# TensorE's last part of the usual path: beside the branch, or behind the general path

## Chip, cores, metric

One core of one Trainium2 chip. The metric is the device time of one execution in microseconds (us); lower is better. Eight executions took 561.7 to 562.5 us at a mean granted clock of 0.997; where a text below says "full clock", these are left out and runs at 0.999 or 1.000 are kept.

## The reference, cut

An adaLN-conditioned block over 2,048 rows of width 512, in bf16: attention (32 query heads of 128, grouped over 8 cached heads, the last 512 keys) and then an MLP. Only the second matters here.

```python
def _B_ref(x, w1, w2):                       # D = 512, Dff = 1792
    h = jnp.einsum('bsd,df->bsf', x, w1)
    h = jnp.maximum(h, zero)
    return jnp.einsum('bsf,fd->bsd', h, w2)
...
h = _layernorm(x, axis=-1) * (1 + cb) + sb
x = x + gb * _B_ref(h, B_w1, B_w2)
```

## The kernel before

The kernel has a fast path, which skips the softmax's maximum, and a general path. During the fast path it works out whether the values were in range: a count of 128 good partitions, written to `flag`. Each engine has a cut in its list of operations; there it waits for the flag, loads it into a register and tests it. With 128 it runs its last part, otherwise the last part and then the general path. TensorE's cut lies in the MLP, ahead of the last two of the four `y_group`s (14 matmuls each) of the second of four blocks of rows.

```python
def emit(self, stream, eng, lo=0, hi=None):
    for fn, waits, incs in stream.ops[lo:hi]:
        for k, c in waits:
            eng.wait_ge(self.sems[k], c)
        ins = fn(eng)
        for k, n in incs:
            ins.then_inc(self.sems[k], n)
...
mlp.extend(lambda b=b, tl=tl: y_group(b - 1, tl) for tl in range(TPB))
if b == NB - 2:
    mlp.insert(len(mlp) - 2, lambda: cut_here("pe"))
    mlp.extend(lambda n=n: cut_here(n) for n in ("dve", "sp", "pool"))
...
# the last y group goes out in three pieces
mlp.extend(lambda a=a: y_group(NB - 1, TPB - 1, *a) for a in
           ((0, D // 2, ACT), (D // 2, 3 * D // 4, SP), (3 * D // 4, D, ACT)))
...
def engine(name, e):
    stream, n_ops = fast[name], cut[name]
    kb.emit(stream, e, 0, n_ops)
    e.wait_ge(sems[flag_ev[0]], flag_ev[1])
    v = e.value_load(flag[0:1, 0:1])
    ...                                # last_part() and rerun(), see the diff
    if name == "pe":
        with e.If(v == 128):
            last_part()                # next to the branch
        with e.Else():
            rerun()                    # the general path
    else:
        with e.If(v != 128):
            rerun()
        with e.Else():
            last_part()                # behind the general path
```

The order of the source is the order of the instructions. So TensorE falls through at the test and has a far jump, over the general path, behind its last matmul; the other four engines jump far at the test (their records of it last 50 to 72 ns) and have the end of the block next to their last part.

Of the kernel before, what the change touches and what calls it, by code (L numbers as in the profile page):

```python
# [1811 lines left out]
def bass_adaLN_cond__sliding_block_cached__dense_activation_relu__prompt_kernel(  # L1812
    nc: bass.Bass,
    A_x: bass.AP,
    A_k_cache: bass.AP,
    A_v_cache: bass.AP,
    A_wq: bass.AP,
    A_wo: bass.AP,
    B_x: bass.AP,
    B_w1: bass.AP,  # L1820
    B_w2: bass.AP,
    c: bass.AP,
    w_mod: bass.AP,
    out: bass.AP,
):
    args = (A_x, A_k_cache, A_v_cache, A_wq, A_wo, B_x, B_w1, B_w2, c, w_mod, out)
    with ExitStack() as top:
        flag = top.enter_context(nc.sbuf_tensor("flag", [1, 8], mybir.dt.int32))
        with ExitStack() as es:
            kb, fast, cut, dma_cnt, flag_ev = build_fast(nc, es, top, *args, flag)  # L1830
            sems = dict(kb.sems)
            meet = top.enter_context(nc.semaphore("s_meet"))
        with ExitStack() as es:
            gkb, general = build_general(nc, es, *args)

            def engine(name, e):
                stream, n_ops = fast[name], cut[name]
                kb.emit(stream, e, 0, n_ops)
                e.wait_ge(sems[flag_ev[0]], flag_ev[1])
                v = e.value_load(flag[0:1, 0:1])  # L1840

                def last_part():
                    kb.emit(stream, e, n_ops)

                def rerun():
                    kb.emit(stream, e, n_ops)
                    if stream.cnt:
                        e.wait_ge(sems[name], stream.cnt)
                    if name == "sp":
                        for k, n in dma_cnt.items():  # L1850
                            e.wait_ge(sems[k], n)
                    e.sem_inc(meet, 1)
                    e.wait_ge(meet, len(fast))
                    gkb.emit(general[name], e)

                if name == "pe":
                    with e.If(v == 128):
                        last_part()
                    with e.Else():
                        rerun()  # L1860
                else:
                    with e.If(v != 128):
                        rerun()
                    with e.Else():
                        last_part()

            with nc.allow_non_contiguous_dma(reason="tiny c vector load in column layout, value rows of 256 bytes"):
                with nc.Block() as block:
                    @block.sync
                    def _(e):  # L1870
                        engine("sp", e)

                    @block.tensor
                    def _(e):
                        engine("pe", e)

                    @block.scalar
                    def _(e):
                        engine("act", e)

                    @block.vector
                    def _(e):
                        engine("dve", e)

                    @block.gpsimd
                    def _(e):
                        engine("pool", e)
    return nc
# [28 lines left out]
```

## Time and profile before

| | kernel before |
|---|---|
| median of 3 runs (range) | 560.84 us (560.29 to 560.89) |
| span of the profiled execution | 558.9 us |
| TensorE busy, granted clock | 98%, 1.0 |
| TensorE's branches | 509.9 us: 90 ns; 554.6 us: 3610 ns |

The time is the device's; the span runs from the first to the last instruction of the profiled execution and is about 2 us shorter.

### The profile page before, as it was taken

Reading aid. Unit: us, or ns where it says so; the run is one execution under the profiler, and the core shown is the slowest. Engines: PE = TensorE matmul, PEld = TensorE weight load, DVE = VectorE, ACT = ScalarE, POOL = GpSimd, SP = SyncE. Lnnn points to the kernel's source line nnn. Section 1 sums busy time; section 2 is a strip of 40 time slices with the busy share of each in tenths; the row PEclk is TensorE's granted clock in tenths of the full one; section 3 lists DMA queues with packets and bytes.
Section 4 is the critical chain, followed back from the end, with each engine's and each line's share of the span. In section 5 each row is a group of like instructions: output and inputs, shape, how many; then the busy total and the mean of one; then the engine's idle time right before and its main releaser. Section 6 shows DMA issues by size and latency. Waiting matters only on the chain.

```text
span 558.9 us, 9675 instructions
## 1 busy us (share of the span) xinstructions
PE 549.5 (98%) x4061; PEld 315.5 (56%) x4135; DVE 254.7 (46%) x555; ACT 349.3 (63%) x453; POOL 53.3 (10%) x50
## 2 busy tenths in 40 slices
PE   8999999999999999999999999999999999999997
PEld 4665555555555555555555555555555554444444
DVE  4455555553546544335445443333354438322134
ACT  5986666666666666666666666666666644432500
POOL 2000022004410000033000000332000000000000
PEclk9999999999999999999999999999999999999999
DMA  9999662522225144353352412121214110200001
GB/s 258 257 203 192 137 162 47 114 43 73 39 41 74 39 84 106 62 129 58 95 95 56 76 40 39 39 38 38 39 39 76 39 29 0 49 28 22 21 29 48
DMA packets 113357, 42.66 MB, mean 76 GB/s; under 512 B 93977, under 2 KB 112153, under 8 KB 113305
## 3 DMA queue, kind: packets, MB, share of 16 engines
q1 hardware_dynamic: 112584, 41.08, 35.5%
q10 hardware_dynamic: 720, 0.89, 0.5%
q8 instruction: 33, 0.54, 0.4%
q14 instruction: 20, 0.16, 0.1%
HBM read 18.35 MB, written 2.10 MB: 37 GB/s over the span
## 4 chain that ended last, share of the span: by engine, by line
PE 97%; issue 1%; DVE 1%; DMA 1%; POOL 0%
PE psS L1374 28%; PE psO L1374 27%; PE psQ L1374 23%; PE psW L1374 19%; DMA x<-in_A_x_dram 1%; DVE st L1384 0%; POOL xn L1613 0%; POOL rstd L1596 0%; DVE mv L1385 0%; DVE qT L1620 0%; PE psS L1377 0%; DVE rstd L1593 0%; DVE PT L1734 0%; DVE PT L1736 0%; DVE tmp L1424 0%
## 5 line engine op out<-in xcount | busy, mean ns | idle before, releaser
L1498 ACT ACTIVATE PT<-psS 128x1024 bf16<-128x1024 f32 x256 | 262.7, 1028 | 128.7 <-PE psS L1374 128.5
L1374 PE MATMUL psS<-qT,kT 128*128 128x512 bf16 x510 | 151.4, 379 | 0.3 <-DVE qT L1620 0.2
L1374 PEld LDWEIGHTS psO<-v,PT 128*128 128x128 bf16 x2048 | 126.6, 98 | 30.2
L1374 PE MATMUL psO<-v,PT 128*128 128x129 bf16 x2048 | 137.0, 220 | 0.0
L1374 PE MATMUL psQ<-hT,wq 128*128 128x512 bf16 (+1 forms) x509 | 130.2, 377 | 0.2
L1508 DVE RECIPROCAL rinv<-psO 128x4 f32<-128x4 f32 x128 | 23.3, 182 | 225.6 <-PE psO L1374 225.6
L1374 PE MATMUL psW<-wo,oT 128*128 128x512 bf16 x452 | 118.1, 379 | 3.1
L1509 DVE TENSOR_TENSOR o<-psO,rinv 128x512 bf16<-128x512 f32 x128 | 88.5, 691 | 4.5
L1374 PEld LDWEIGHTS psQ<-hT,wq 128*128 128x128 bf16 x512 | 49.9, 98 | 59.8 <-DVE qT L1488 0.4
L1374 PEld LDWEIGHTS psS<-qT,kT 128*128 128x128 bf16 x512 | 49.6, 98 | 58.8 <-ACT PT L1498 0.5
L1490 ACT ACTIVATE qT<-psQ 128x512 bf16<-128x512 f32 x125 | 74.1, 593 | 0.0
L1723 ACT ACTIVATE wq<-psS 128x512 bf16<-128x512 f32 x56 | 33.4, 597 | 49.1 <-PE psS L1374 49.1
L1374 PEld LDWEIGHTS psW<-wo,oT 128*128 128x128 bf16 x512 | 44.9, 98 | 32.9 <-DVE acc L1531 1.2
L1531 DVE TENSOR_TENSOR acc<-psW,acc 128x512 f32<-128x512 f32 x48 | 33.2, 691 | 6.7 <-PE psW L1374 6.7
L1374 PE MATMUL psO<-wmw,wq 128*128 128x512 bf16 (+1 forms) x165 | 32.8, 352 | 0.2
L1534 POOL TENSOR_TENSOR acc<-acc,gaf 128x512 f32<-128x512 f32 x12 | 15.6, 1301 | 146.8 <-DVE acc L1531 139.8
L1390 POOL TENSOR_TENSOR rstd<-rstd,cst 128x4 f32<-128x4 f32 x7 | 7.2, 1025 | 215.7 <-DVE rstd L1389 215.7
L1734 DVE TENSOR_TENSOR PT<-psO,gbf 128x512 f32<-128x512 f32 (+1 forms) x12 | 7.5, 624 | 40.4 <-PE psO L1374 40.4
L1374 PE MATMUL psS<-h2T,wmw 128*128 128x512 bf16 x110 | 25.2, 379 | 0.1
L1374 PEld LDWEIGHTS psO<-wmw,wq 128*128 128x128 bf16 x168 | 15.3, 98 | 16.6
L1374 PE MATMUL psS<-hT,wmw 128*128 128x512 bf16 x110 | 24.4, 379 | 0.1
L1384 DVE BATCH_NORM_STATS2 st<-x 128x6 f32<-128x512 bf16 x31 | 21.1, 680 | 3.6 <-DMA x<-in_A_x_dram 3.6
(90 smaller groups left out, 192.0 us busy)
## 6 DMA issues: line engine op xcount, KB each, us to landing
wo<-in_A_wo_dram SPq DMA_DIRECT2D x4, 1024.0 KB, 6.5
wq<-in_A_wq_dram SPq DMA_DIRECT2D x7, 512.0 KB, 4.6
wmw<-in_B_w_dram SPq DMA_DIRECT2D x14, 256.0 KB, 3.1
wmw<-in_w_mod_dram SPq DMA_DIRECT2D x4, 512.0 KB, 5.1
oT<-o SPq DMA_TRANSPOSE x128, 2.4
out_dram<-PT SPq DMA_DIRECT2D x15, 128.0 KB, 1.7
x<-in_A_x_dram SPq DMA_DIRECT2D x3, 512.0 KB, 4.4
v<-in_A_v_cache_dram SPq DMA_DIRECT2D x8, 128.0 KB, 4.1
```

The lines of the kernel that those rows point to most:

```text
L1374: kb.op(PE, lambda e: e.matmul(out_ap, lhsT, rhs, start=start, stop=stop), reads=reads, group_writes=[R_b[k] for k in bk], signal=signal)
L1384: kb.op(DVE, lambda e: e.bn_stats(st[:, t, :], x_sb[:, t, :]), reads=[R_x[t]], writes=[R_st[t]])
L1390: kb.op(POOL, lambda e: e.tensor_tensor(rstd[:, sl], rstd[:, sl], cst[:, 0:1].to_broadcast([P, hi - lo]), op=ALU.pow), reads=R_rstd[sl] + ...
L1490: kb.op(ACT, lambda e: e.activation(qT[u % NQT][:, :], bank[bk], ACTF.Copy), reads=[R_b[bk]], writes=[R_qT[u % NQT]])
L1498: kb.op(ACT, lambda e: e.activation(PT[u % NPT][:, pr * 2:pr * 2 + 2, :], s_ps[pr][:, :, :], ACTF.Exp, scale=scale), reads=[R_b[pr * 2], R ...
L1508: kb.op(DVE, lambda e: e.reciprocal(rinv[:, u, :], o_ps[:, :, P]), reads=[R_b[5], R_b[6]], writes=[R_rinv])
L1509: kb.op(DVE, lambda e: e.tensor_tensor(o_sb[u % NOS][:, :, :], o_ps[:, :, 0:P], rinv[:, u, :].unsqueeze(2).to_broadcast([P, TPB, P]), op=A ...
L1531: kb.op(DVE, lambda e: e.tensor_tensor(acc[:, tl, :], bank[WBK], acc[:, tl, :], op=ALU.add), reads=[R_b[WBK], R_acc[tl]], writes=[R_acc[tl]])
L1534: kb.op(eng, lambda e: e.tensor_tensor(acc[:, tl, :], acc[:, tl, :], gaf[:, :], op=ALU.mult), reads=[R_acc[tl], R_ga], writes=[R_acc[tl]])
L1723: kb.op(ACT, lambda e: e.activation(h1T[b % 2][:, fc, :], bank[bk], ACTF.Relu), reads=[R_b[bk]], writes=[R_h1[b % 2][fc]], pre=all_events( ...
L1734: kb.op(DVE, lambda e: e.tensor_tensor(yt[i][:, c0:c1], bank[bk][:, c0:c1], gbf[:, c0:c1], op=ALU.mult), reads=[R_b[bk], R_gb], writes=[R_ ...
```

## The change

Its intent is a simpler program: TensorE gets the same layout as the others. The usual path then pays for one far jump of TensorE in the MLP, and for none at the end.

```diff
--- before.py
+++ after.py
@@ -1838,11 +1838,7 @@
                 kb.emit(stream, e, 0, n_ops)
                 e.wait_ge(sems[flag_ev[0]], flag_ev[1])
                 v = e.value_load(flag[0:1, 0:1])
-
-                def last_part():
-                    kb.emit(stream, e, n_ops)
-
-                def rerun():
+                with e.If(v != 128):
                     kb.emit(stream, e, n_ops)
                     if stream.cnt:
                         e.wait_ge(sems[name], stream.cnt)
@@ -1852,17 +1848,8 @@
                     e.sem_inc(meet, 1)
                     e.wait_ge(meet, len(fast))
                     gkb.emit(general[name], e)
-
-                if name == "pe":
-                    with e.If(v == 128):
-                        last_part()
-                    with e.Else():
-                        rerun()
-                else:
-                    with e.If(v != 128):
-                        rerun()
-                    with e.Else():
-                        last_part()
+                with e.Else():
+                    kb.emit(stream, e, n_ops)
 
             with nc.allow_non_contiguous_dma(reason="tiny c vector load in column layout, value rows of 256 bytes"):
                 with nc.Block() as block:
```

No arithmetic, wait or transfer of data changes; the list of TensorE's instructions before and behind the branch is the same in both kernels.

## The prediction

Where a cut is marked, a passage is gone: on how instructions are stored and fetched, on the depth of a queue, and on the clock. The forecast's sum: 0.99 + 1.0 + 1.37 = 3.36 us of jump, or 3.61 as measured, gives a gap of 0.21 or 0.46 us, 0.35 is chosen, and 560.84 + 0.35 = 561.2 us. Part (a), why the target must be fetched: for that stand only the packets that the trace has behind the far branches (the one inside the jump at the end: 16 KB, 1.25 us).

> **What bounds the kernel now.** I read the page first: engine totals, then the chain that ended last.
>
> ```profile
> PE 549.5 (98%) x4061; PEld 315.5 (56%) x4135; DVE 254.7 (46%) x555; ACT 349.3 (63%) x453; POOL 53.3 (10%) x50
> PEclk9999999999999999999999999999999999999999
> PE 97%; issue 1%; DVE 1%; DMA 1%; POOL 0%
> ```
>
> TensorE is busy 98% of 558.9 us at an undiminished clock, and 97% of the chain of waits is its own matmuls. So any time in which its array really runs dry goes straight into the end, and nothing that only delays another engine by a microsecond matters. The change touches one place on TensorE: the test of the flag inside the MLP. So I next read the instructions of the flag, of the lines of the two branches, and of the block's end (columns: line, engine queue, operation, count, durations in ns as min/median/max, first and last start in us).
>
> ```profile
> L1840 PEldq TENSOR_LOAD <-flag x1: 488/488/488, 509.4 to 509.4; - x1
> L1857 PEldq COMPARE_BRANCH  x2: 90/1850/3610, 509.9 to 554.6; - x2
> L1862 ACTq COMPARE_BRANCH  x1: 50/50/50, 508.2 to 508.2; - x1
> L1862 DVEq COMPARE_BRANCH  x1: 72/72/72, 520.8 to 520.8; - x1
> L1862 SPq COMPARE_BRANCH  x1: 53/53/53, 521.9 to 521.9; - x1
> L1868 PEldq DRAIN  x1: 68/68/68, 558.3 to 558.3; - x1
> L1868 SPq DRAIN  x1: 13/13/13, 558.6 to 558.6; - x1
> ```
>
> TensorE has two branches now. The first, at 509.9 us, is not taken: it falls through into the last part and takes 90 ns. The second, at 554.6 us, is the jump over the general path to the end of the block, and its record lasts 3610 ns. That is a far jump of this very engine, measured in this very kernel, only at a place where it stands beside the drain of the last results. The last row but one and the last show that TensorE arrives at the end at 558.3 us and SyncE, which waits for the last output, at 558.6 us: the far jump of today costs nothing, by 0.3 us.
>
> Third, the timeline of TensorE around the test (start, length, engine, instructions).
>
> ```profile
> 506.97 5.93 PEld L1374 LDWEIGHTS psO<-wmw,wq 128*128 128x128 bf16 x28
> 507.18 6.21 PE L1374 MATMUL psO<-wmw,wq 128*128 128x512 bf16 x27
> 513.01 2.04 PEld L1374 LDWEIGHTS psQ<-wmw,wq 128*128 128x128 bf16 x10
> 513.23 2.10 PE L1374 MATMUL psQ<-wmw,wq 128*128 128x512 bf16 x9
> ```
>
> The load and the branch at 509.4 to 510.0 us leave no trace on the array. It works through 28 matmuls of psO without a gap until 513.23 us, and only then comes psQ, the first matmul behind the branch. So the sequencer is ahead of the array: when it reads the flag (509.363 us in the trace), the array has (513.228 - 509.363) / 0.216 = 18 matmuls to go, 3.87 us. The same lead of some 18 matmuls is there at the end of the kernel, where a matmul of 128 columns starts every 56 ns: (555.75 - 554.62) / 0.056 = 20. So the lead is a queue that is full, and the sequencer can fill it at 28 ns an instruction or faster.
>
> [...]each far branch is followed by a packet of the instruction queues, and TensorE's record of 3610 ns contains one.[...]the trace shows a lead of 18 pairs of weight load and matmul, 36 instructions, and I use the 36.[...]
>
> **The change, part by part.** No arithmetic, wait, load of the flag or transfer of data changes. Three things do.
>
> (a) The branch at 509.9 us is now taken, and its target lies behind the general path. Counted in the compiled program of the kernel before, TensorE's general path has 5,942 instructions and its last part 448[...].
>
> (b) The jump at the end goes: the last part now lies next to the end of the block. 3.61 us of sequencer time disappear, but from a place with 0.3 us less than SyncE's arrival. Gain: 0.
>
> (c) The other four engines already have this layout, and stay.
>
> The cost of (a) is the far jump less the lead. The jump I take apart with the instruction packets, by windows of the DMA view (queue, packets, MB, share of 16 engines' time in the window): the first line is the window 555.6 to 557, the second 510.97 to 511.9, an ordinary fetch in sequence with little traffic beside it.
>
> ```profile
> q8 instruction: 1, 0.02, 5.6%
> q8 instruction: 1, 0.02, 6.2%
> ```
>
> A share times 16 times the window is the packet's time: 0.056 x 16 x 1.4 = 1.25 us, and 0.062 x 16 x 0.93 = 0.92 us. The packet of the far jump started at 555.61 us, 0.99 us after the branch did (554.62), landed at 556.86, and the record ended at 558.23, 1.37 us later. The other engines have the same first step (from their branch to a packet on their instruction queue: DVE 1.02 us, SyncE 0.96 us, ACT 0.99, POOL 1.37), so it is the jump and not the drain of TensorE's queue that sets it. In the middle of the MLP the packet should be like the ordinary ones, most of which take 0.92 to 1.15 us. Sum: 0.99 + 1.0 + 1.37 = 3.36 us; or, as measured once, 3.61.
>
> The branch starts at 509.915. The sequencer goes on at 509.915 + 3.36 = 513.28 (513.53 with the other figure). Between the end of the jump at the kernel's end and the next instruction 0.06 us pass, and a weight load takes 98 ns, so psQ's first matmul can start at 513.28 + 0.06 + 0.10 = 513.44 (513.69). It started at 513.228. **The array runs dry for 0.21 us (0.46 us)**; everything else of the 3.4 us lies under the 15 matmuls in the queue. I choose 0.35, between the two.
>
> Behind it nothing is regained: the last part is one chain of matmuls at 216 ns, and the tail (last eviction, last output, SyncE's waits) shifts with it. The queue refills, since 28 ns an instruction is well below the 108 ns at which the array takes one. The prediction is 560.84 + 0.35 = 561.2 us.
>
> **The rivals.**
>
> First: the lead hides it wholly. If the fetch comes back faster (a packet of 0.9 us, or a resume in less than 1.37 us because that step held something of the kernel's end), the jump takes under 3.2 us and the change costs nothing: 560.8 us. For it: the margin is only 0.2 us. Against: the only jump of this engine that was measured took 3.61 us.
>
> Second: a second fetch on top. [...]in the kernel before, the fetch in sequence began at 510.98, just 1 us behind the branch. If the sequencer has that block already under way when it jumps, the wanted packet stands behind a useless one of about 1 us, and the loss is 0.35 + 1.0: 562.2 us. ACT's jump shows two packets in a row (508.83 and 509.17), which may be just this.[...]
>
> Third: no lead, the whole jump exposed, since the sequencer must drain before it branches: 560.84 + 3.6 = 564.4 us[...]. Against it: in the kernel before, the load and branch ran 3.2 us ahead of the array, and the packet at the end began at its usual 1.0 us.
>
> Fourth: a gain from the end, if TensorE's arrival there were what the others wait for. Against it: SyncE arrives 0.3 us later, and it waits for the last output, which ACT issued at 556.45 us, after VectorE; 560.84 or better is not expected from this.
>
> **Range and chances.** The runs of the kernel before spread from 560.29 to 560.89, so half a microsecond is noise. The first rival gives 560.5 to 560.9, the main line 561.0 to 561.4, the second up to 562.2. I weigh them 0.25, 0.5 and 0.15, with a rest of 0.1 for the third and the unknown. A range of 560.5 to 562.2 holds the most of it. Two per cent are 11.2 us, three times a whole far jump: same is almost certain.
>
> **What would show it.** Right: TensorE has one far branch, at 509.9 us, of 3.3 to 3.6 us, with one instruction packet of 16 KB starting about 510.9; psQ's first matmul starts 0.2 to 0.5 us after the psO group has ended, where there was no gap; TensorE reaches the drain of the end near 556 us instead of 558.3; SyncE still ends last. Wrong: no gap at all (first rival); two packets of the instruction queue before psQ (second); a gap of over 3 us[...] (third); or an end that comes earlier relative to the last matmul (fourth).

## More of the kernel before

A change of the time by tenths of a microsecond is to be read from two stretches of the span: the MLP around 510 us, and the tail, from VectorE's last write (556.42 us) to the last instruction. The prediction shows the lines of the first. In the second, the outputs leave in pieces; the following lines are the last pieces in the DMA view of the kernel before (output, queue of the issuing engine, operation, count, KB, us from issue to landing).

```profile
out_dram<-PT SPq DMA_DIRECT2D x15, 128.0 KB, 1.7
out_dram<-PT ACTq DMA_DIRECT2D x1, 64.0 KB, 2.7
out_dram<-PT SPq DMA_DIRECT2D x1, 32.0 KB, 2.4
out_dram<-PT ACTq DMA_DIRECT2D x1, 32.0 KB, 1.9
```

A piece of 128 KB lands in 1.7 us (a median of 15), and the later piece of half the size takes 2.7.

## The result

| | before | changed |
|---|---|---|
| median of 6 runs (range) | 560.75 us (560.29 to 560.90) | 560.69 us (560.46 to 560.85) |
| span of the profiled execution | 558.855 us | 558.965 us |

The ratio is 1.0, with a 95% interval of 0.9987 to 1.0012: the same. (A ratio is the mean time of one kernel's fast runs over that of the other's of the same rounds, so not quite the ratio of the medians quoted.) The time is inside the predicted range, 0.5 us under the predicted value. The profile says that this equality has two parts that were not both foreseen.

The lines of the branches and the block's end, changed kernel:

```profile
L1841 PEldq COMPARE_BRANCH  x1: 3860/3860/3860, 509.8 to 509.8; - x1
L1841 ACTq COMPARE_BRANCH  x1: 50/50/50, 508.1 to 508.1; - x1
L1855 PEldq DRAIN  x1: 1195/1195/1195, 555.2 to 555.2; - x1
L1855 SPq DRAIN  x1: 13/13/13, 558.7 to 558.7; - x1
```

The far jump has moved to 509.8 us and takes 3.86 us. TensorE now reaches the end at 555.2 us (its drain lasts until 556.4), SyncE as before last, at 558.7. The timeline of TensorE around the branch, changed kernel (in brackets the idle time of the row's first instruction):

```profile
506.90 5.92 PEld L1374 LDWEIGHTS psO<-wmw,wq 128*128 128x128 bf16 x28
513.75 1.19 PEld L1374 LDWEIGHTS psQ<-wmw,wq 128*128 128x128 bf16 x7 [0.93 <-issue]
507.11 6.21 PE L1374 MATMUL psO<-wmw,wq 128*128 128x512 bf16 x27
513.76 1.47 PE L1374 MATMUL psQ<-wmw,wq 128*128 128x512 bf16 x6 [0.44 <-issue]
```

There is a hole where the kernel before had none. The row's 0.44 us is counted from the modelled end of a matmul (379 ns); in a stream a matmul starts every 216 ns, so by starts the hole is 513.758 - (512.938 + 0.216) = 0.604 us. I use this measure below and call it the gap. Everything behind it comes 0.54 us later than before (VectorE's last write ends at 556.96 instead of 556.42 us; the stretch ahead of the branch had come 0.07 us earlier). But the span grew by only 0.11 us. The rest is given back in the tail, which took 2.438 us before and takes 2.005 us now. The last pieces of the output, changed kernel:

```profile
out_dram<-PT SPq DMA_DIRECT2D x15, 128.0 KB, 1.7
out_dram<-PT ACTq DMA_DIRECT2D x1, 64.0 KB, 1.6
out_dram<-PT SPq DMA_DIRECT2D x1, 32.0 KB, 1.5
out_dram<-PT ACTq DMA_DIRECT2D x1, 32.0 KB, 1.5
```

All three land sooner, the 64 KB by 1.1 us. The DMA view of the kernel before for the window 554.5 to 558.8 us has one line that the changed kernel's tail lacks:

```profile
q8 instruction: 1, 0.02, 1.8%
```

It is the block of instructions that the far jump at the end fetched, 16 KB in one packet, from 555.609 to 556.856 us, inside the record of the jump (554.616 to 558.226 us). Each piece of the output has 16 reports in the trace, and its landing is the sixteenth. Of the 64 KB piece, 15 reports came by 556.705 us and the sixteenth at 557.884, 1.18 us later; in the changed kernel all 16 came between 557.069 and 557.247. So I formed a **theory**: the packet of the jump held one of the DMA engines, the output's share on that engine stood behind it, and SyncE, which waits for all outputs, ended later. The traces don't name the DMA engine of a packet, so that it is one engine, held until the packet ends, stays a theory. What the trace shows fits it: one packet of 1.25 us beside those of the 64 KB piece with a median of 0.03 us. It also shows the share that waited. The 64 KB piece is 128 packets of 512 B. In the kernel before, 120 of them start by 556.329 us; the other eight, a sixteenth of the piece, start one after another from 556.842 to 557.252 us, as the instruction packet ends (556.856). The last eight packets of the next piece follow only behind these, from 557.307 us. In the changed kernel all 128 start between 556.543 and 556.869 us. The DMA view of the kernel before from 556.83 to 557.31 us has these eight, and the report behind them, on the queue of that piece:

```profile
q10 hardware_dynamic: 9, 0.00, 7.3%
```

One part stays open. The last piece of all has its 16 reports together in the kernel before (558.200 to 558.362 us); what made it late there is that ACT's issue of it took 0.78 us instead of 0.35. Why that issue took longer is not shown.

### The profile page after: what moved, and what is told of

The parts are those of the page before. It is cut to its first block, busy times and chain, and to the rows that moved or that the text cites. A ratio compares the mean times of both kernels' runs of the same rounds, so it can differ in the third digit from the quotient of the medians.

```text
span 559.0 us, 9673 instructions
## 1 busy us (share of the span) xinstructions
PE 550.4 (98%) x4060; PEld 315.7 (56%) x4135; DVE 254.7 (46%) x555; ACT 349.4 (63%) x453; POOL 53.3 (10%) x50
## 4 chain that ended last, share of the span: by engine, by line
PE 97%; issue 1%; DVE 1%; DMA 1%; POOL 0%
PE psS L1374 28%; PE psO L1374 27%; PE psQ L1374 22%; PE psW L1374 19%; DMA x<-in_A_x_dram 1%; DVE st L1384 0%; POOL xn L1613 0%; POOL rstd L1596 0%; DVE mv L1385 0%; DVE qT L1620 0%; PE psS L1377 0%; DVE rstd L1593 0%; DVE PT L1734 0%; DVE PT L1736 0%; DVE tmp L1424 0%
```

## The experiments

Two theories are tested. One: **gap = jump + 0.06 us - lead**, where the lead is how long the array still has work when the branch starts. Two: **the packet of the end costs 0.4 us in the tail**. Against the first stands that a restarted array needs some fixed time, or that the lead hides the jump and the gap was chance; against the second, that tails differ from run to run.

All profiles in one table. "First" is from the branch's start to the instruction packet's, "rest" from the packet's end to the branch's end; all in us. The medians are those of the runs of full clock, beside the kernel before on the same chip.

| run | jump: first + packet + rest = total | lead | gap | tail | median (before) |
|---|---|---|---|---|---|
| before | 0.99 + 1.25 + 1.37 = 3.61, at the end | | 0 | 2.438 | |
| changed | 1.51 + 0.99 + 1.35 = 3.86 | 3.316 | 0.604 | 2.005 | 560.69 (560.75) |
| e0 changed again | 1.01 + 1.43 + 1.36 = 3.80 | 3.308 | 0.551 | 2.002 | 560.68 (560.78) |
| e8 changed, third | 1.20 + 0.93 + 1.44 = 3.56 | 3.309 | 0.314 | 2.002 | 560.53 (560.71) |
| e1 early flag | 0.99 + 1.04 + 1.51 = 3.54 | 3.866 | 0 | 1.997 | 560.19 (560.78) |
| e7 early flag again | 0.98 + 1.17 + 1.54 = 3.70 | 3.866 | 0 | 2.003 | 560.47 (560.71) |
| e9 early flag, third | 0.98 + 1.03 + 1.45 = 3.46 | 3.866 | 0 | 2.004 | 560.30 (560.71) |
| e2 early flag, near | 1.47 + 0.96 + 1.36 = 3.79, at the end | | 0 | 2.463 | 560.70 (560.78) |
| e3 two jumps | 1.01 + 1.24 + 1.37 = 3.62; at the end 3.58 | 3.311 | 0.364 | 2.369 | 560.64 (560.78) |
| e4 two loads | 0.99 + 1.25 + 1.36 = 3.60 | 2.810 | 0.853 | 2.002 | 561.01 (560.71) |
| e5 late jump | 0.97 + 1.12 + 1.37 = 3.45, at the end | | 0 | 3.844 | 562.33 (560.71) |
| e6 cut earlier | 1.52 + 0.98 + 1.52 = 4.02 | 3.316 | 0.761 | 2.629 | 561.21 (560.71) |

Every verdict is "same", and only e5's interval (ratio 1.0016 to 1.0047) leaves out 1.0. So the sizes of the two effects are read from the profiles, of which there is one for each run. Span less gap less tail is 556.26 to 556.57 us in eleven of the twelve, and 556.79 in e6: the two terms account for the spans to about 0.3 us, but for e6.

### e0 and e8: the changed kernel again

No edit.

> The changed kernel once more, unedited, so that the others have it beside them on one chip. Theory (two effects that cancel): the far jump in the MLP leaves TensorE's array dry for 0.60 us (513.154 to 513.758 us in the first trace of it), and the far jump that is gone from the end had cost 0.43 us there, because its instruction packet held one DMA engine while the last outputs were written (one of the 16 landings of the output before the last came 1.18 us after the other 15). Time of before plus 0 to 0.2 us. Rival (the lead hides the jump and the gap of the trace is a chance of one execution): the gap is not there again, or not of this size, and the tail is as in before.

> The changed kernel, unedited, on one chip with the next. Both effects predict: gap at the branch of 0.35 to 0.65 us, tail 2.00 us, time within 0.2 us of before.

The gap is there in all three profiles, 0.604, 0.551 and 0.314 us, and the tail is 2.00 us in each; the third gap is a little below what I expected. The rival that the lead hides the jump falls. The gaps follow the jump's length to the hundredth: 3.80 + 0.06 - 3.308 = 0.55, and 3.563 + 0.06 - 3.309 = 0.31. This says no more than that psQ starts 0.06 us after the jump ends, each time; whether the lead counts is tested by e1 and e4.

### e1, e7 and e9: the flag loaded earlier, in the changed kernel

The wait for the flag and the load go 14 matmuls up; the branch stays.

```diff
-                    mlp.insert(len(mlp) - 2, lambda: cut_here("pe"))
+                    mlp.insert(len(mlp) - 3, lambda: cut.update(load=len(PE.ops)))
+                    mlp.insert(len(mlp) - 2, lambda: cut_here("pe"))
...
-                kb.emit(stream, e, 0, n_ops)
+                n_load = cut["load"] if name == "pe" else n_ops
+                kb.emit(stream, e, 0, n_load)
                 e.wait_ge(sems[flag_ev[0]], flag_ev[1])
                 v = e.value_load(flag[0:1, 0:1])
+                kb.emit(stream, e, n_load, n_ops)
```

> The changed kernel with TensorE's wait for the flag and its load of the flag moved 14 matmuls up, one y group ahead of the branch; the branch stays where it is. The load's 0.55 us then no longer comes out of the lead at the branch: lead 18 matmuls, 3.87 us, against a jump of 3.86 us. Theory: the gap falls from 0.60 us to 0.0 to 0.15 us, the tail stays as in the changed kernel, time about 0.5 us under the changed kernel and 0.4 us under before (560.3 us). Rival (the gap is the restart of the array after a jump and not jump less lead): the gap stays near 0.6 us and the time is that of the changed kernel.

> The early load of the flag in the changed kernel once more, on this chip and in other rounds, as the candidate that beats both kernels: no gap at the branch, tail of 2.00 us, 0.4 to 0.6 us under before.

> The early load of the flag in the changed kernel, a third set of rounds, to settle the size of its gain: the two profiles of it say 0.44 us under before and 0.55 to 0.6 us under the changed kernel (no gap, tail 2.00 us); the timings so far gave 0.6 and 0.2 us under before. Expected 0.3 to 0.6 us under before in the runs of full clock.

The load and the branch of TensorE in the first of the three:

```profile
L1842 PEldq TENSOR_LOAD <-flag x1: 491/491/491, 506.4 to 506.4; - x1
L1844 PEldq COMPARE_BRANCH  x1: 3537/3537/3537, 509.4 to 509.4; - x1
```

Its timeline behind them:

```profile
513.28 1.89 PE L1374 MATMUL psQ<-wmw,wq 128*128 128x512 bf16 x8
```

The jump still takes over 3.5 us, but the lead at the branch is 3.866 us, as the queue had time to fill again behind the load; psQ follows psO without idle time. No fixed restart is seen, so the rival of the first theory falls. In time the three sets give 0.59, 0.24 and 0.41 us under before (medians at full clock; of the second, 0.4 to 0.6 was expected) and, on the chips where the changed kernel ran too, 0.49 and 0.23 us under that. The profiles say 0.44 (the tail 2.44 less 2.00). The ratios keep the runs at 0.997 (four of the eleven of the kernel before beside the first set). Their intervals each reach past 1.0 (0.9989, 0.9973 to 1.0005; 1.0002, 0.9989 to 1.0016; 0.9993, 0.9979 to 1.0006), and the second is over 1.0 itself. So timing alone does not settle the gain. The medians at full clock have the same direction three times, and in the third set all five runs (560.13 to 560.35 us) lie under all nine of the kernel before (560.43 to 560.85). By these medians it is the fastest version found, by 0.04 to 0.11%. The fit is tight: by the same sum a jump of 4.02 us, as in e6, would leave a gap of 0.21 us.

### e2: the flag loaded earlier, in the kernel before

The same edit on the kernel before.

> The same early load in the kernel before, where the last part lies next to the branch. Theory: the load was hidden there already, nothing changes: time of before within 0.15 us, no gap at the branch, and one of the 16 landings of the next-to-last output again 1 us late at the end. If moving the load gains something by itself, it shows here.

As expected: 0.08 us under before, no gap, and a tail of 2.463 us. Again one report of the 64 KB piece was late, at 557.918 us after 15 by 556.543. The early load gains nothing by itself. One detail differs: ACT's last issue of an output took 0.35 us here and 0.78 us in the kernel before, with nearly equal tails; here the last piece's own sixteenth report was late instead (558.232 us, after 15 by 557.772). So that longer issue, which I had taken for part of the cause, isn't needed for the loss.

### e3: a far jump at both places

```diff
                 with e.Else():
                     kb.emit(stream, e, n_ops)
+                    if name == "pe":
+                        with e.If(v != 128):
+                            gkb.emit(general[name], e)
```

> The changed kernel with a second far jump of TensorE put back at the end: behind its last part stands the general path once more, under a condition that is never true there. Theory: gap of 0.6 us as in the changed kernel, and at the end again one of 16 landings about 1 us late, ACT's last issue of an output at 0.7 to 0.8 us instead of 0.35, the tail from VectorE's last write to the end 0.4 us longer: time 0.4 us over the changed kernel, 0.5 us over before (561.2 us). Rival (the tails differ by chance): tail and time as in the changed kernel.

TensorE's branches:

```profile
L1841 PEldq COMPARE_BRANCH  x1: 3616/3616/3616, 509.8 to 509.8; - x1
L1854 PEldq COMPARE_BRANCH  x1: 3577/3577/3577, 554.9 to 554.9; - x1
```

The last pieces of the output in the DMA view:

```profile
out_dram<-PT ACTq DMA_DIRECT2D x1, 64.0 KB, 2.7
out_dram<-PT SPq DMA_DIRECT2D x1, 32.0 KB, 2.4
out_dram<-PT ACTq DMA_DIRECT2D x1, 32.0 KB, 1.8
```

The profile has both effects, the gap (0.364 us) and the long tail (2.369 us), and a sixteenth report 1.14 us late. The slow landings come back with the jump, so it is not chance that they were gone. The median time does not show it: 560.64 us instead of the 561.2 I expected, 0.04 us under the changed kernel of the same rounds. A shorter gap in this execution accounts for 0.2 us of it; the rest is within what single runs scatter by (560.38 to 561.17 us), and stays unexplained. The two profiled executions do show it: the span is 559.08 us here and 558.91 in e0, 0.17 us more, where gap and tail together are 0.18 us longer.

### e4: a second load ahead of the branch

```diff
                 v = e.value_load(flag[0:1, 0:1])
-                with e.If(v != 128):
+                bad = v != 128
+                if name == "pe":
+                    bad = v + e.value_load(flag[0:1, 0:1]) != 256
+                with e.If(bad):
```

> The changed kernel with TensorE's flag loaded twice in a row ahead of the branch (the sum of both is tested), which takes one more load and one register addition, about 0.5 to 0.65 us, off the lead at the branch. Theory (gap = jump + what stands ahead of it, less the lead): the gap grows from 0.55 to 0.60 us by that amount to 1.0 to 1.25 us, tail as in the changed kernel at 2.00 us, time 0.55 us over the changed kernel (561.2 to 561.3 us). Rival (the array waits for the restart and not for the lead): gap unchanged at 0.55 to 0.6 us.

The second load, the addition and the branch:

```profile
L1843 PEldq TENSOR_LOAD <-flag x1: 308/308/308, 509.9 to 509.9; - x1
L1844 PEldq ALU_OP  x1: 44/44/44, 510.3 to 510.3; - x1
L1844 PEldq COMPARE_BRANCH  x1: 3602/3602/3602, 510.4 to 510.4; - x1
```

The timeline behind them:

```profile
514.06 1.25 PE L1374 MATMUL psQ<-wmw,wq 128*128 128x512 bf16 x5 [0.69 <-issue]
```

The lead shrank from 3.31 to 2.81 us and the gap is 3.602 + 0.06 - 2.810 = 0.85 us; measured 0.853. It is less than the 1.0 to 1.25 I expected, because the jump was 0.26 us shorter than in the trace I had added to, and the load took 0.31 instead of 0.49 us. The time is 0.30 us over before (ratio 1.0007, 0.9992 to 1.0022); the gap (0.85) less the tail's gain (0.44) would give 0.41. The tail is that of the changed kernel. With e1 this is the lead varied in both directions.

### e5: the jump at the end later, in the kernel before

```diff
                         last_part()
+                        e.wait_ge(sems["dve"], fast["dve"].cnt)
                     with e.Else():
                         rerun()
```

> The kernel before with TensorE made to wait for VectorE's last result ahead of its far jump at the end. Theory (the packet of the jump holds one DMA engine while outputs are written): the packet now starts about 1 us after VectorE's end, at 557.5 us, so the output before the last and the one ahead of it land all 16 within 0.2 us, ACT's last issue takes 0.35 us, and if anything it is the last output that has one late landing; TensorE itself becomes the last to arrive, 3.6 us behind VectorE, and the tail grows from 2.44 to about 4.2 us: time about 562.5 us. Rival (the first of the last outputs is late for a reason of its own, such as its two writers): its 16th landing stays 1.1 us late.

The last pieces of the output:

```profile
out_dram<-PT ACTq DMA_DIRECT2D x1, 64.0 KB, 1.5
out_dram<-PT SPq DMA_DIRECT2D x1, 32.0 KB, 1.5
out_dram<-PT ACTq DMA_DIRECT2D x1, 32.0 KB, 3.1
```

The arrivals at the block's end:

```profile
L1869 SPq DRAIN  x1: 13/13/13, 559.9 to 559.9; - x1
L1869 PEldq DRAIN  x1: 68/68/68, 560.0 to 560.0; - x1
```

The packet now runs from 557.444 to 558.562 us, and the delay moves with it: the two earlier pieces land in 1.5 us, and the last one, until now 1.9 us, takes 3.1 (15 reports by 557.946 us, the sixteenth at 559.590). The rival that the 64 KB piece is late for a reason of its own falls. And TensorE itself is now the last at the end, by 0.13 us over SyncE: its jump, 3.45 us from 556.478 us on, is covered by the outputs only in part. The tail is 3.844 us (about 4.2 expected), the time 1.6 us over before.

### e6: the branch 14 matmuls earlier

```diff
-                    mlp.insert(len(mlp) - 2, lambda: cut_here("pe"))
+                    mlp.insert(len(mlp) - 3, lambda: cut_here("pe"))
```

> The changed kernel with TensorE's branch one y group (14 matmuls, 3.0 us) earlier in its stream, so elsewhere in a block of instructions. Theory: the lead is 18 matmuls there too, gap of 0.35 to 0.65 us, time and tail as in the changed kernel. If the first step of the jump depends on where in its block the branch stands (1.5 us in the first trace of the changed kernel, 1.0 us in the others), the branch comes out at 3.3 us and the gap near zero.

TensorE's branch:

```profile
L1841 PEldq COMPARE_BRANCH  x1: 4017/4017/4017, 507.3 to 507.3; - x1
```

The instruction queue in the DMA view from 556 to 558 us, then the last pieces of the output:

```profile
q8 instruction: 1, 0.02, 5.3%
```

```profile
out_dram<-PT ACTq DMA_DIRECT2D x1, 64.0 KB, 3.1
out_dram<-PT SPq DMA_DIRECT2D x1, 32.0 KB, 2.7
out_dram<-PT ACTq DMA_DIRECT2D x1, 32.0 KB, 2.1
```

This came out otherwise than I expected: 0.50 us over before (four runs from 560.57 to 562.05 us; ratio 1.0006, 0.9991 to 1.0021). The longer jump, 4.02 us, makes a gap of 0.761. And without any jump at the end an instruction packet stands there, from 556.277 to 557.978 us, with all three pieces late, the 128 KB piece ahead of them too (its sixteenth report came 2.19 us after the fifteenth), and a tail of 2.629 us. No far jump of TensorE stands there, and the span has 34 packets on that queue, q8, where the changed kernel's has 33. The branch standing 14 matmuls earlier makes TensorE's last part 28 instructions longer, and as the path through the general code contains a copy of it, the whole program too: 14,299 instead of 14,271. By my estimate, the changed kernel's 33 packets for some 8,330 instructions (14,271 less the 5,942 that are jumped over) are one for about 250, so a shift by 28 can put the last instructions into one packet more; that this is the cause is not shown. I had not thought of it, but it is a second way to bring a packet to the outputs; the tail is 0.63 us longer with it than without. (The profiled execution, 562.05 us, was the slowest of the four; the flag was already 0.4 us later in it than in the changed kernel, so this part has nothing to do with the branch.) The question whether the first step depends on the branch's place in its block (in what one packet of 16 KB brings) is not settled: 1.5 us here and once in the changed kernel, but 1.0 and 1.2 us in two other executions of that same program.

## Why the prediction was right, and where not

The time lay in the stated range, and "same" came true. That it did is in part luck: the cost at the branch was 0.3 to 0.6 us, for 0.35 predicted, and at the end, where the gain was put at 0, 0.43 us came back. By its steps:

- **What bounds the kernel**: right. A hole in TensorE's array went into the end in full: VectorE's last write moved by 0.54 us, for a gap of 0.60 and a start 0.07 us earlier.
- **Jump less lead**: the mechanism was right, shown by the lead varied from 2.81 to 3.87 us in e1 and e4. The size was somewhat off: 0.35 us predicted (0.2 to 0.5 in its list of signs, with a jump of 3.3 to 3.6), 0.60, 0.55 and 0.31 us in the three profiles of the changed kernel. The mis-sized term is the jump, 3.36 to 3.61 us in the sum and 3.86, 3.80 and 3.56 measured; its first step was 1.51 us instead of 0.99 in the one trace, its packet 1.43 us instead of 1.0 in the other. Another term was wrong the other way: no 0.10 us for a weight load, as psQ's first matmul starts 4 ns after its weight load.
- **"Gain: 0" for the jump that goes from the end**: this is the step that failed. I compared when TensorE and SyncE arrive, and saw 0.3 us in hand. Whether SyncE arrives late because of the jump's packet I did not ask, though the DMA view of the kernel before had a 64 KB output landing in 2.7 us beside 1.7 for those of 128 KB. The runs show 0.43 us (tail 2.438 and 2.463 us with the jump, 1.997 to 2.005 in the seven profiles without a packet there).
- **The fourth rival** was turned down for the same reason and was partly what happened, though not in the way it was put: TensorE's arrival was not what the end waited for. The sign that the prediction had named for it, an end that comes earlier relative to the last matmul, did appear: 2.88 us after that matmul's start instead of 3.31.
- **The first rival**, no cost since the lead covers all, has the number nearest the result (560.8 us). But its mechanism is refuted; the equality is a cost of 0.3 to 0.6 us and a gain of 0.43.
- **The second rival**, a useless packet ahead of the wanted one, was not seen: one packet of TensorE's queue (q8) between branch and psQ in each profile. **The third**, the jump fully exposed, fell too: the gap is 0.3 to 0.6 us and not 3.6.
- **Instructions counted**: the 5,942 that it gives to the general path are all that the jump passes over, the copy of the last part among them; the distance is as it says.

## What to carry to other kernels

A far jump took TensorE's sequencer 3.45 to 4.02 us in these runs (13 records, mean 3.66), and all of it was free in the three where it was issued with 18 matmuls of 512 columns still ahead of it (3.87 us, the longest lead seen): so do what eats the lead, such as loading the condition (0.55 us here), some matmuls earlier (14 here) and keep it in a register. When a piece of control flow is moved, ask also what its instruction fetch collided with at the old place; near the last outputs a single 16 KB packet came with one landing of 16 late by 1.1 to 2.2 us (five profiles), and the end was later by 0.4 to 0.6 us (in four of them; in e5 TensorE's own wait adds to it). Of the engines' rows at most ACT's showed it (an issue of 0.63 to 0.78 us instead of 0.35 in three of the five profiles); the landings in the DMA view showed it each time. And where a change "costs nothing", check whether that is one zero or two terms: here, taking both apart gave a version with neither cost in its three profiles.
